# Out stages of an attention and MLP kernel: score tiles in 16 bursts of three and two in place of 18 of two, two and three

## The chip, the cores and the metric

The kernel runs on one core of a Trainium2 chip. The metric is the device time of one execution in microseconds (us); a time given for a kernel is the median of its runs. TensorE does the matmuls, ScalarE (ACT) the activations, VectorE (DVE) elementwise work, GpSimd (POOL) mainly issues loads, and the queue of SyncE (SP) issues transposes and stores. Each engine takes its instructions in program order and waits for others by semaphores. Matmul results land in PSUM, which has eight banks.

## What is computed

Sigmoid attention over 8 batches and 12 heads (448 rows, head size 64), and behind it a two-layer MLP with a SiLU over the 3584 rows of width 768:

```python
scores = scale * np.matmul(q, k.transpose(0, 1, 3, 2)) - np.log(S)
attn = 1.0 / (1.0 + np.exp(-scores))
attn_out = np.matmul(attn, v)
x = attn_out.transpose(0, 2, 1, 3).reshape(B * S, H * D)
h = x @ w_in                                # 768 -> 2048
g = h * (1.0 / (1.0 + np.exp(-h)))
return g @ w_out                            # 2048 -> 768
```

## The kernel before

Four heads of one batch make a group, so there are 24 groups (`g`), three to a batch. A group has seven score tiles (`NCH`), and a tile is one row block of 64 rows of k for four heads: `scores(g, ch)` (L218) issues four 64x64 matmuls of 448 columns, one on each quadrant of the array, into a pair of PSUM banks `psc`, and one sigmoid of ScalarE (L232) takes the pair out to `attnT` in SBUF. Two heads share a bank on its two partition halves. The sigmoids of a group's seven tiles are then multiplied with its values: `values(g)` (L240) issues 28 matmuls of the same small kind into a pair of banks `pav`, and VectorE takes the pair out with two `tensor_scalar_mul` (L267), one for each bank. These are called the two scales below.

The program goes: the first 24 tiles with transposes and values; the first MLP layer of batches 0 and 1 with tiles 24 to 41 in it; then for m = 0, 1, 2 an out stage and an h stage; and a last out stage without scores. An out stage `sets(m)` multiplies the hidden rows of batches 2m and 2m+1 with `w_out`. Each set is seven products of eight dense 128x128 matmuls of 384 columns (L504), by a Strassen-like scheme with sums `S` and evictions on VectorE (L512 to L539). There are three sets in stages 0 and 2 and four in stage 1 (and in the last). In between these dense matmuls the out stage computes all 42 score tiles and five of the six values products for the next two batches. The sixth values product (of the group that ends with the stage's last tile) stands at the beginning of the h stage, `h_pair`, which multiplies the new rows with `w_in`.

The order of TensorE's work in an out stage is fixed when the program is built. `burst(n, size)` (L738) issues `size` score tiles in a row and behind them, if a group is complete and waiting, its values. A group is put on `waiting` after the burst that holds its seventh tile, so its values come with the next burst. Then comes a number of dense matmuls taken from the stream `sets(m)`. The planner keeps a running sum `left` in ns: each burst adds its share of the stage's planned time and takes off its own cost (200 for a burst, `SWITCH`, 200 for each tile, 1330 for values), and the rest is filled with dense matmuls at 163 each, at least one:

```python
left += total * size / (2 * NT_B) - SWITCH - TILE * size - VALUES * burst(n, size)
count = max(1, round(left / DENSE))
```

With sizes 2, 2, 3 in turn (L773), seven tiles take three bursts; every complete group ends with a burst of three, and the values go along with the next burst of two. After each burst and again in the middle of its dense matmuls `rows_if_any` (L589) may issue one further step of side work: a VectorE copy and a transpose on SP's queue for the k or q of a later group, or a sum over x.

PSUM in these stages (`banks_for_attention(3)`, L766) is three double pairs, taken in turn, and two single banks for the dense products (`po`). Score tiles and the values' `pav` both take the next double pair (`two_banks`, L96). `reuse_waits="tile"` in `new_pool` makes the first write to a pair wait for the readers of the tile that had it before.

Of the kernel before, what the change touches and what calls it, by code (L numbers as in the profile page):

```python
# [17 lines left out]
def kernel(  # L18
# [18 lines left out]
    NQ = NPAIR // 2  # L37
    NT_B = NQ * NCH
# [25 lines left out]
    def banks_for_attention(doubles):  # L64
        psum.close()
        banks.clear()
        bufs_of.update(double=doubles, single=NBANK - 2 * doubles)
        for name, bufs in bufs_of.items():
            taken[name] = 0
            new_pool(name, bufs)  # L70
# [7 lines left out]
    def banks_for_h():  # L78
        doubles = [[2 * i, 2 * i + 1] for i in longest_idle("double")]
        ring[:] = sum(doubles[:-2], [])  # L80
        ring.extend(2 * bufs_of["double"] + i for i in longest_idle("single"))
        ring.extend(sum(doubles[-2:], []))
        psum.close()
        banks.clear()
        new_pool("any", 1)
        for i in range(NBANK):
            banks[i] = banks["any"].tile([P, 512], F32, tag=f"any{i}", name=f"any{i}")
# [130 lines left out]
    def scores(g, ch):  # L218
        attnT[g, ch] = p12.tile([P, 2, S], F16, tag="attnT", name="attnT")
        psc = two_banks("psc")  # L220
        for half in range(2):
            own = slice(half * HP, (half + 1) * HP)
            for j in range(2):
                rows = slice(j * D, (j + 1) * D)
                nc.tensor.matmul(  # L225
                    psc[own, j, :S],
                    qkT["k", g][rows, ch, own],
                    qkT["q", g][rows, :, own],
                    start=True,
                    stop=True,  # L230
                )
        nc.scalar.activation(attnT[g, ch], psc[:, :, :S], AF.Sigmoid, bias=bias_s, scale=QKSCALE)  # L232
# [7 lines left out]
    def values(g, end=NCH):  # L240
        b, iq = divmod(g, NQ)
        if b not in xT:
            assert b < 2 or b - 2 in h_done
            xT[b] = p2.tile([P, NPAIR, S], F16, tag="xT", name="xT")
        pav, done_rounds = part_of.pop(g, None) or (None, 0)
        if pav is None and bufs_of["double"] > 2 and "any" not in banks:
            both = two_banks("pav")
            pav = [both[:, half] for half in range(2)]
        elif pav is None:
            pav = [one_bank("pav") for _ in range(2)]  # L250
        for ch in range(done_rounds, end):
            at = attnT.pop((g, ch))
            for half in range(2):
                own = slice(half * HP, (half + 1) * HP)
                for j in range(2):
                    nc.tensor.matmul(  # L256
                        pav[half][j * D : (j + 1) * D, :S],
                        flat["v", g][own, j, ch, :],
                        at[own, j, :],
                        start=(ch == 0),  # L260
                        stop=(ch == NCH - 1),
                    )
        if end < NCH:
            part_of[g] = pav, end
            return
        for half in range(2):
            nc.vector.tensor_scalar_mul(xT[b][:, half * NQ + iq, :], pav[half][:, :S], SX)  # L267
        if iq == NQ - 1:
            ready.add(b)
# [75 lines left out]
    def x_sums(m, lo, hi):  # L345
        if lo == 0:
            for i in (1, 2, 4):
                tx[m, i] = room_x()
        of = slice(lo, hi)
        x0, x1 = ([xT[2 * m + j][:, c * NQ : (c + 1) * NQ] for c in range(2)] for j in range(2))  # L350
        for o, x, y in (
            (tx[m, 1], x1[0], x0[0]),
            (tx[m, 2], x1[1], tx[m, 1]),
            (x1[0], x1[1], x1[0]),
            (tx[m, 4], x0[1], tx[m, 2]),
        ):
            nc.vector.tensor_sub(o[:, of], x[:, of], y[:, of])
            yield
# [211 lines left out]
    def sets(m):  # L570
        for g in range(0, NCH - 1, 2):
            step = out_set(
                block(m, g), row_blocks(m, g), block(m, g + 1), row_blocks(m, g + 1)
            )
            for i, ns in enumerate(step):
                if m == 0 and g == 0 and i in (10, 14):
                    next(sums)
                if m == 0 and g == 0 and i in (20, 28, 36, 44):
                    next(in_sums)
                yield ns  # L580
        if m % 2 == 1:
            g = NCH - 1
            yield from out_set(
                kept, row_blocks(m - 1, g), block(m, g), row_blocks(m, g), m == B // 2 - 1
            )
# [3 lines left out]
    def rows_if_any(before, copy):  # L589
        if sums_of_x and next(sums_of_x[0], "end") == "end":  # L590
            sums_of_x.pop()
        if later and later[0][0] < before:
            g, name = later.pop(0)
            dma_transpose(g, name, copy)
            if name == "q":
                behind_rows(g, before)
# [48 lines left out]
    def after_values(g):  # L645
        if g == 0:
            load("v", 3)
            load_w_in(2)
            load_w_in(3)
        elif g == 1:  # L650
            load("v", 4)
            load_w_out(0, 0)
            load_w_out(0, 1)
        elif g == 2:
            load("v", 5)
            load_w_out(1, 0)
            load_w_out(1, 1)
            load("kq", 6)
            load("kq", 7)
        elif g + 3 < NQB:  # L660
            load("v", g + 3)
        if g >= 2 * NQ and g % (2 * NQ) == 2 * NQ - 2:
            sums_of_x.append(x_sums(g // (2 * NQ), 0, NQ - 1))

    def values_if_any():
        if waiting:
            g = waiting.pop(0)
            values(g)
            after_values(g)
            return True  # L670
        return False
# [66 lines left out]
    def burst(n, size=2):  # L738

        new = units[n : n + size]  # L740
        for u in new:
            scores(*u)
        with_values = values_if_any()
        for g, ch in new:
            if ch == NCH - 1:
                waiting.append(g)
                if 9 <= g + 3 < NQB:
                    later.extend(((g + 3, "k"), (g + 3, "q")))
        return with_values
# [3 lines left out]
    for n in range(NT_B + 3, 2 * NT_B, 2):  # L753
        burst(n)
        if n in (26, 30):
            transposes(5, "k" if n == 26 else "q")
        stretch(stream, 1600)
# [6 lines left out]
    SWITCH, TILE, VALUES, DENSE = 200, 200, 1330, 163  # L764
    for m in range(B // 2 - 1):
        banks_for_attention(3)  # L766
        nc.scalar.activation(warm, bias_s, AF.Sigmoid)
        stream = sets(m)
        for _ in range(FIRST_DENSE):
            next(stream)  # L770

        dense = (3 + m % 2) * 7 * NHC - FIRST_DENSE - ENDING
        sizes = [2, 2, 3]  # L773
        costs = sum(SWITCH + TILE * size for size in sizes) * 2 * NQ + VALUES * (2 * NQ - 1)
        total = dense * DENSE + costs
        own = 2 * NQ * (m + 2)
        left, n = 0.0, 2 * NT_B * (m + 1)
        for size in sizes * (2 * NQ):
            left += total * size / (2 * NT_B) - SWITCH - TILE * size - VALUES * burst(n, size)
            n += size  # L780
            rows_if_any(own, nc.vector.tensor_copy)
            count = max(1, round(left / DENSE))
            left -= count * DENSE
            half = count // 2
            for i in range(count):
                next(stream)
                if i == half:
                    rows_if_any(own, nc.vector.tensor_copy)
        assert not sums_of_x
        nc.scalar.activation(warm, bias_s, AF.Silu)  # L790
        for _ in stream:
            pass
        (g,) = waiting
        waiting.clear()
        banks_for_h()
        values(g, NCH - 1)

        def last_values():
            values(g)
            after_values(g)  # L800
            for _ in x_sums(m + 1, NQ - 1, NQ):
                pass
            nc.gpsimd.tensor_copy(gate, tx[m + 1, 4][:1, NQ - 1, :1])

        for i, _ in enumerate(h_pair(m + 1, last_values)):
            if i % 8 == 7:
                rows_if_any(NQB, nc.gpsimd.tensor_copy)
# [33 lines left out]
```

## Time and profile before

| | us |
|---|---|
| median of 3 runs | 369.92 (369.61 to 370.37) |
| the profiled execution | 369.69 |
| its span, first to last instruction | 367.7 |
| out stage 0 (m = 0), to the first matmul of the h stage | 48.4, from 75.57 |
| out stage 1 (m = 1) | 57.1, from 156.27 |
| out stage 2 (m = 2) | 48.5, from 245.61 |
| last out stage, without scores | 41.1, from 326.6 |

In the profile a line of the timeline has start and duration in us, the engine, the line of the kernel, the operation, what it writes and reads, its size, and how many such instructions in a row were merged; in brackets is the idle time ahead of it and what ended that. A matmul's record is longer than the distance to the next one's start (dense ones last 0.33 us in the records and follow each other after 0.163), so how long a stretch takes is read from starts. The costliest groups of the three out stages in the table of groups are the sigmoids (168 of 1009 ns, over the whole kernel), the dense products `po` and the score matmuls `psc`; the scales are 48 instructions of 620 ns over the whole kernel, of which each of the three out stages has ten.

### The profile page before, as it was taken

How to read it: one execution, taken by the hardware profiler on the slowest of the kernel's cores; microseconds unless marked ns; L12 is line 12 of the kernel's file. 1: busy time of each engine (PE TensorE's matmuls, PEld its weight loads, DVE VectorE, ACT ScalarE, POOL GpSimd, SP SyncE). 2: the span in 40 equal slices, each digit the busy share in tenths (PEclk: the TensorE clock that was granted, in tenths of full speed). 3: DMA queues.
4: the chain of work that ended last, by engine and by line, in shares of the span. 5: the costliest groups of instructions: out<-in, count | busy, mean ns of one | idle time of the engine just before them, and what ended most of it. 6: DMA issues, size and time to landing. Idle time of an engine off the chain costs nothing. (4 is left out here: it accounts for less than half of the span.)

```text
span 367.7 us, 7596 instructions
## 1 busy us (share of the span) xinstructions
PE 359.5 (98%) x3009; PEld 183.2 (50%) x3009; DVE 251.9 (68%) x458; ACT 249.9 (68%) x339; POOL 77.8 (21%) x116
## 2 busy tenths in 40 slices
PE   7999999999999999999999999999999999999995
PEld 2554445545544555544444545554455545555553
DVE  2565569867657587867665758795756667797763
ACT  5998885479998755687777846679998856640000
POOL 8566521040060172000051047000100000000000
PEclk9999999999999999999999999999999999999999
DMA  8999999989969499007589369912863020003333
GB/s 142 200 202 202 204 204 203 187 116 141 164 100 227 110 128 180 2 0 166 92 165 206 61 128 144 128 15 51 153 111 86 21 69 0 3 0 86 87 86 86
DMA packets 65698, 42.78 MB, mean 116 GB/s; under 512 B 36096, under 2 KB 62208, under 8 KB 65664
## 3 DMA queue, kind: packets, MB, share of 16 engines
q0 software_dynamic: 27072, 22.58, 42.3%
q1 hardware_dynamic: 38240, 19.44, 26.8%
q8 instruction: 23, 0.38, 0.4%
q10 hardware_dynamic: 352, 0.30, 0.2%
q14 instruction: 11, 0.09, 0.1%
HBM read 45.61 MB, written 11.01 MB: 154 GB/s over the span
## 5 line engine op out<-in xcount | busy, mean ns | idle before, releaser
L232 ACT ACTIVATE attnT<-psc,bias_s 128x896 f16<-128x896 f32 x168 | 158.1, 1009 | 21.9 <-PE psc L225 21.6
L504 PEld LDWEIGHTS <-S 128*128 128x128 f16 x448 | 41.3, 98 | 36.5 <-issue 8.1
L225 PE MATMUL psc<-qT,kT 64*64 64x448 f16 x672 | 51.1, 362 | 1.5 <-ACT qT L186 0.6
L267 DVE TENSOR_SCALAR xT<-pav 128x448 f16<-128x448 f32 x48 | 27.7, 620 | 33.2 <-PE pav L256 33.2
L124 POOL DMA_DIRECT2D vf<-in_v_dram x24 | 17.2, 717 | 135.0 <-PE pav L256 120.9
L504 PEld LDWEIGHTS <-gTr 128*128 128x128 f16 x336 | 31.3, 98 | 26.6 <-issue 7.7
L504 PE MATMUL po<-T,S 128*128 128x384 f16 x224 | 42.0, 327 | 0.2 <-DVE S L515 0.2
L504 PE MATMUL po<-w_out_sb,gTr 128*128 128x384 f16 x224 | 41.6, 327 | 0.0
L378 PEld LDWEIGHTS <-w_in_sb 128*128 128x128 f16 x288 | 27.7, 98 | 26.9 <-issue 1.7
L504 PE MATMUL po<-w_out_sb,S 128*128 128x384 f16 x224 | 40.8, 326 | 0.0
L256 PE MATMUL pav<-attnT,vf 64*64 64x448 f16 x672 | 38.9, 350 | 0.5 <-DVE gTr L303 0.4
L288 PE MATMUL ph<-xT,w_in_sb 128*128 128x448 f16 x192 | 38.7, 353 | 0.1
L378 PE MATMUL pa<-xT,w_in_sb 128*128 128x448 f16 x144 | 33.2, 353 | 0.0
L225 PEld LDWEIGHTS <-kT 64*64 64x64 f16 x672 | 17.8, 104 | 28.8 <-issue 22.3
L378 PEld LDWEIGHTS <-SI 128*128 128x128 f16 x216 | 21.1, 98 | 20.0 <-issue 0.5
L256 PEld LDWEIGHTS <-vf 64*64 64x64 f16 x672 | 21.0, 106 | 14.0 <-issue 4.7
L288 PEld LDWEIGHTS <-w_in_sb 128*128 128x128 f16 x192 | 17.8, 98 | 19.1 <-issue 3.7
L394 ACT ACTIVATE part<-pa 128x448 f32<-128x448 f32 x24 | 13.1, 544 | 19.9 <-PE pa L378 19.0
L504 PE MATMUL po<-T,gTr 128*128 128x384 f16 x112 | 22.1, 327 | 0.0
L372 ACT ACTIVATE gTr<-pc 128x448 f16<-128x448 f32 x24 | 13.1, 544 | 12.9 <-DVE pc L388 12.5
L388 DVE TENSOR_TENSOR part<-pb,part 128x448 f32<-128x448 f32 x24 | 14.9, 621 | 8.3 <-ACT part L394 5.0
L186 ACT ACTIVATE m<-po 128x384 f32<-128x384 f32 x1 | 0.5, 491 | 27.7 <-PE po L504 27.7
(75 smaller groups left out, 467.7 us busy)
## 6 DMA issues: line engine op xcount, KB each, us to landing
out_dram<-osb SPq DMA_DIRECT2D x54, 192.0 KB, 3.0
vf<-in_v_dram POOLq DMA_DIRECT2D x24, 224.0 KB, 7.0
kf<-in_k_dram POOLq DMA_DIRECT2D x23, 224.0 KB, 7.7
qf<-in_q_dram POOLq DMA_DIRECT2D x23, 224.0 KB, 7.9
w_in_sb<-in_moe_w_in_dram POOLq DMA_DIRECT2D x16, 192.0 KB, 8.2
w_out_sb<-in_moe_w_out_dram POOLq DMA_DIRECT2D x4, 768.0 KB, 14.9
kT<-kr SPq DMA_TRANSPOSE x18, 4.1
qT<-qr SPq DMA_TRANSPOSE x18, 4.8
```

The source lines that it names most:

```text
L124: nc.gpsimd.dma_start(flat[name, g][:, :, c0:c1].rearrange("p i c d -> p i (c d)"), rows_in(name, g)[:, :, c0 * D : c1 * D],)
L186: nc.scalar.activation(o, i, AF.Copy)
L225: nc.tensor.matmul(psc[own, j, :S], qkT["k", g][rows, ch, own], qkT["q", g][rows, :, own], start=True, stop=True,)
L232: nc.scalar.activation(attnT[g, ch], psc[:, :, :S], AF.Sigmoid, bias=bias_s, scale=QKSCALE)
L256: nc.tensor.matmul(pav[half][j * D : (j + 1) * D, :S], flat["v", g][own, j, ch, :], at[own, j, :], start=(ch == 0), stop=(ch == NCH - 1),)
L267: nc.vector.tensor_scalar_mul(xT[b][:, half * NQ + iq, :], pav[half][:, :S], SX)
L288: nc.tensor.matmul(ph[:, :S], w_in_sb[:, cc, fc * P : (fc + 1) * P], xT[b][:, cc, :], start=(at == 0), stop=(at == NCC - 1),)
L372: nc.scalar.activation(gTr[:, r * NG + i, col + c * S : col + (c + 1) * S], h, AF.Silu, bias=0.0, scale=ISX)
L378: nc.tensor.matmul(to, w[:, n, i * P : (i + 1) * P], x[:, n], start=(start and n == 0), skip_group_check=not start, stop=(n == NQ - 1),)
L388: nc.vector.tensor_add(o, po, x)
L394: nc.scalar.activation(got[i, 1], bank[i, "a"], AF.Copy)
L504: nc.tensor.matmul(po[:, :NO2], a[:, fc, :], w[:, fc, :], start=(fc == 0), stop=(fc == NHC - 1))
```

## The change

The sizes of the bursts in an out stage are written out for the whole stage: ten bursts of three and six of two, 16 in all, across the limits of the groups. The complete groups' last tiles lie in bursts 3, 5, 8, 11, 13 and 16; the values go along with bursts 4, 6, 9, 12 and 14, which are bursts of two, and each of these five is followed by a burst of three. An assertion in `burst` says that values go along with two tiles alone. The planner's costs count 16 bursts in place of 18; its constants and its rule are the same, and so are all matmuls, activations and copies in number.

```diff
@@ burst
         with_values = values_if_any()
+        assert not with_values or size == 2
@@ out stage
         dense = (3 + m % 2) * 7 * NHC - FIRST_DENSE - ENDING
-        sizes = [2, 2, 3]
-        costs = sum(SWITCH + TILE * size for size in sizes) * 2 * NQ + VALUES * (2 * NQ - 1)
+        sizes = [3, 3, 3, 2, 3, 2, 3, 3, 2, 3, 3, 2, 3, 2, 3, 2]
+        assert sum(sizes) == 2 * NT_B
+        costs = sum(SWITCH + TILE * size for size in sizes) + VALUES * (2 * NQ - 1)
         total = dense * DENSE + costs
         own = 2 * NQ * (m + 2)
         left, n = 0.0, 2 * NT_B * (m + 1)
-        for size in sizes * (2 * NQ):
+        for size in sizes:
```

## The prediction

> **What bounds the kernel now.** I read the page first, for the share of each engine, then the windows over the three stages that the change touches, then the timeline of TensorE inside such a stage, and then the timeline of all engines around one values product.
>
> ```profile
> PE 359.5 (98%) x3009; PEld 183.2 (50%) x3009; DVE 251.9 (68%) x458; ACT 249.9 (68%) x339; POOL 77.8 (21%) x116
> ...
> 75.57:123.98 48.41, 48.41 (x501) 24.53 (x499) 33.21 (x61) 43.21 (x47) 11.41 (x17) 1.00 0.89 146
> 156.27:213.32 57.05, 56.90 (x558) 28.20 (x556) 38.32 (x70) 43.93 (x49) 8.41 (x12) 1.00 0.61 114
> 245.61:294.14 48.53, 48.53 (x502) 24.47 (x500) 32.07 (x58) 43.87 (x49) 2.15 (x3) 1.00 0.42 80
> ```
>
> TensorE is busy all through, at a granted clock of 1.00 in these stages, and the chain of waits that ended last is TensorE work almost alone. The three windows are the out stages: length first, then the busy time of TensorE, weight load, VectorE, ScalarE and GpSimd, the granted clock, and the DMA. A busy TensorE hides short waits, because a matmul record here is longer than its pitch, so starts have to be compared. Whatever TensorE loses or gains in these windows goes into the end time one for one.
>
> The price of a burst comes from two undisturbed ones of the second out stage:
>
> ```profile
> 156.27 2.44 PE L504 MATMUL po<-w_out_sb,gTr 128*128 128x384 f16 x14
> 158.64 0.57 PE L225 MATMUL psc<-qT,kT 64*64 64x448 f16 x8
> 159.15 0.50 PE L504 MATMUL po<-w_out_sb,gTr 128*128 128x384 f16 x2
> ...
> 162.82 0.98 PE L504 MATMUL po<-T,gTr 128*128 128x384 f16 x5
> 163.72 0.76 PE L225 MATMUL psc<-qT,kT 64*64 64x448 f16 x12
> 164.42 0.66 PE L504 MATMUL po<-T,gTr 128*128 128x384 f16 x3
> ```
>
> Eight score matmuls are two tiles, twelve are three. A dense matmul follows the last after 0.163 us (2.44 less one record of 0.33, over 13). So the two-tile burst costs 159.15 - 156.27 - 14 x 0.163 = 0.60, and the three-tile burst 164.42 - 162.82 - 5 x 0.163 = 0.79. That gives 0.19 for a tile and 0.22 for the burst itself. Of the burst, 0.09 lies ahead of its first matmul, and from there to the next dense matmul it is 0.51 (two tiles) or 0.70 (three).
>
> The stretch around a values product in the third out stage:
>
> ```profile
> 262.44 0.57 PE L225 MATMUL psc<-qT,kT 64*64 64x448 f16 x8
> ...
> 262.84 1.49 PE L256 MATMUL pav<-attnT,vf 64*64 64x448 f16 x28
> 262.93 1.91 ACT L232 ACTIVATE attnT<-psc,bias_s 128x896 f16<-128x896 f32 x2 [0.39 <-PE psc L225]
> ...
> 264.27 0.34 PE L504 MATMUL po<-w_out_sb,gTr 128*128 128x384 f16 x1
> 264.39 1.16 DVE L267 TENSOR_SCALAR xT<-pav 128x448 f16<-128x448 f32 x2 [1.04 <-PE pav L256]
> ...
> 264.53 0.74 PE L225 MATMUL psc<-qT,kT 64*64 64x448 f16 x8
> ...
> 265.21 0.66 PE L504 MATMUL po<-w_out_sb,gTr 128*128 128x384 f16 x3
> ...
> 267.11 2.81 ACT L232 ACTIVATE attnT<-psc,bias_s 128x896 f16<-128x896 f32 x3 [0.17 <-PE psc L225]
> ```
>
> After the values there is one dense matmul and at once the next burst. Its body is 265.21 - 264.53 = 0.68 and not 0.51: the second tile waits 0.17 until ScalarE has emptied its banks (262.93 + 1.91 = 264.84). VectorE's two scales empty the values' banks from 264.39 to 265.55. Those banks are next wanted by the first tile of the three-tile burst, at 266.61, a whole 1.06 us later. That distance is what the change takes away.
>
> **The change part by part.** *Fewer bursts.* 18 become 16 in each of three stages, with the same 42 tiles, values and dense matmuls: 6 x 0.22 = -1.32 us.
>
> *Old waits that go.* The two-tile bursts after values in the first and third out stage have bodies of 0.61, 0.67, 0.67, 0.68, 0.67 and 0.61, 0.68, 0.67, 0.68, 0.68 by their starts (0.51 undisturbed): 0.75 + 0.77. Three three-tile bursts there are above 0.70 by 0.10, 0.16 and 0.05. In all 1.83 us; the second out stage has none. They all disappear, or are contained in the new wait below: -1.83.
>
> *The new wait.* Three double banks A, B, C go round in turn. Before, a group of seven tiles took 2 + values, 2, 3, which is eight banks, so the values' pair was followed by two other pairs before it came up again. Now every burst with or without values takes exactly A, B, C: scores in A and B, values in C, and the burst right behind it, three tiles, takes C for its third tile. In the changed program's order the first matmul of that third tile holds a wait on VectorE's second scale, behind all five values of each stage. Reckon from the dense matmul behind the values (264.27 above). The next burst begins at +0.26, its third tile would begin at +0.26 + 2 x 0.19 = +0.64. The scales begin at +0.12, take 1.16, and the word of VectorE reaches TensorE some 0.06 later (estimate: from the end of ScalarE's 264.84 to the weight load that waited for it, 264.89, 0.05; and 0.07 in the second stage between a VectorE sum's end and the product that waited for it). So the third tile begins at +1.34: a wait of 0.70. How many dense matmuls follow a burst is fixed at build time by the planner's running sum `left`, which charges 1330 ns for the values: still a single one behind each of the five in the first and third out stage: 10 x 0.70 = 7.0. The second has three dense matmuls there four times, and four once. Its rows put the burst at +0.59 (from 177.94 to 178.53) and +0.76 (from 169.11 to 169.87), so the third tile is due at +0.97 and +1.14 and waits 0.37 and 0.20: 4 x 0.37 + 0.20 = 1.68. Added: +8.68. TensorE takes its work in order, so the dense matmuls behind the tile are all late with it; the product evictions and S sums of VectorE behind the scales are no later relative to them.
>
> This rests on VectorE being free when the values end. In the rows of before it had idled 0.7 to 2.4 us ahead of nearly all scales. In the new order the VectorE work ahead of each pair is at most an eviction, an S sum and a copy for a transpose (0.56 + 0.68 + 0.61 = 1.85), whose product ended at least before the burst that carries the values, 0.40 + 1.42 = 1.8 us. I take no delay, and keep up to 0.61 (one more piece) at a few of the fifteen for the upper end.
>
> The Trainium skill speaks against this edit: Perfetto Trace Analysis, Optimizing Tensor Performance (Matmuls), has independent matmul groups rotate through different PSUM banks, so that one is evacuated under the next one's matmuls. Here the rotation continues but falls in step with the bursts. The trace agrees as to the old order (the 1.06 us above); the page prices nothing, so by it only the sign follows.
>
> *ScalarE in rows of three.* The first eviction starts 0.49 after a burst's first matmul (262.44 to 262.93) and three take 2.81, with 0.06 for the word to TensorE; so the third pair is free at +3.36. With 13 dense matmuls the next burst starts at 0.70 + 13 x 0.163 + 0.09 = +2.91 and wants it at +3.29: 0.07 late once per such stage, and 0.04 late once ahead of values. With 14 there is no wait, and behind a stalled burst there is slack. +0.22 over the first and third stage; the bounds are 0 and 0.24 for each of some four bursts with 12 or 13 dense matmuls, 2 us in all. In the second stage there are 17 or 18 and none waits.
>
> *The moved calls.* The 36 places per stage at which copies for transposes and sums of x are issued become 32, all still ahead of their need: a group's k and q copies follow its predecessor's last tile by no more than a burst, with some 10 us before the scores that read them, and the transposes land in 4 to 5 us. SP's and POOL's queues get the same issues in the same order: 0, covered by those 10 us; if the cover were gone, one landing (4.8) would be exposed.
>
> Sum: -1.32 - 1.83 + 8.68 + 0.22 = **+5.75 us**. The profiled execution took 369.69 (span 367.7 and 2.0 around it), which gives 375.4; the median of the runs is 0.23 above it, so I say **375.6 us**.
>
> **The rivals.** *The faster side: the third tile is let in after the first scale.* A tile's first matmul writes the first bank of the pair, the second scale only reads the other. If the wait really ended there, at +0.12 + 0.62 + 0.06 = +0.80, it would cost 0.16 ten times and nothing in the second stage: -1.32 - 1.83 + 1.6 + 0.22 = -1.3, 368.6 us. It decides as soon as the fifteen waits total under 2.9 us instead of 8.7. For it: the halves lie in different banks. Against it: the wait in the built order is on the second scale. 5%.
>
> *The loss is half given back.* TensorE's pauses let VectorE and ScalarE catch up, and waits inside dense stretches (0.15 on an S sum in the second stage) vanish, or the third tile's weights and queue start sooner. With 0.50 instead of 0.70: 2 to 3 us less, 373. Against it: dense stretches show hardly any wait to be given back. 10%.
>
> *VectorE comes late to the scales.* One piece of 0.61 at each of five values: +3.1, 378.7 us; at all fifteen 384.8. For it: VectorE is busy two thirds of these stages (33.21 of 48.41 us in the first) and the copies stand close. Against it: the idle time ahead of the scales. 10%.
>
> *A burst removed saves nothing*, because the 0.22 is from two rows and may belong to the tiles: 376.9, inside the range; 5%.
>
> **How the numbers follow.** The forecast itself, 374 to 377.5, has 67%. What is left, 3%, is that losses and gains cancel. The range takes in the half loss and the VectorE case at five values: 372.5 to 379. A difference of 0.2% (0.74 us) is about what a measurement of this kernel tells from none: faster by more 5%, within it 3%, slower 92%.
>
> **What would show it.** In the timeline after, each burst behind values has twelve score matmuls over some 1.4 us to the next dense matmul in the first and third out stage, and 0.9 to 1.1 in the second, with VectorE's scale named as the releaser of the third tile; the three windows grow by about 2.3, 1.2 and 2.2 us; all other three-tile bursts have bodies near 0.70. I am wrong if these bodies are near 0.7 to 0.8, or if the windows grow elsewhere, in the dense products or between the stages.

## The result and the profile after

The changed kernel takes 375.51 us (median of 4 runs, 375.05 to 375.68), the kernel before 370.02 in the same comparison: a ratio of 1.0147 (95% interval 1.0135 to 1.0159), 5.49 us slower. The forecast was 375.6.

The windows of the three out stages in the profile after, with the same columns as before:

```profile
76.00:126.77 50.77, 49.04 (x501) 24.21 (x500) 33.28 (x61) 43.00 (x47) 11.15 (x17) 1.00 0.82 139
159.06:216.96 57.90, 57.23 (x558) 28.52 (x556) 38.45 (x70) 43.71 (x49) 8.04 (x12) 1.00 0.64 112
249.24:300.01 50.77, 49.10 (x502) 24.29 (x500) 32.06 (x58) 43.71 (x49) 2.14 (x3) 1.00 0.41 76
```

Against 48.41, 57.05 and 48.53 they are longer by 2.36, 0.85 and 2.24 us, 5.45 together; the forecast had 2.3, 1.2 and 2.2. The span grew by 5.9 (373.6 against 367.7): the remaining 0.43 is there before the first out stage, which begins at 76.00 and not 75.57. It arises in the first 7 us, in code that did not change (the first score matmul starts at 7.03 and not 6.60); in the profiles of all versions here, which do not differ up to that stage, its start lies between 75.17 and 76.19.

The timeline of all engines around one values product and the burst behind it in the third out stage, from the profile after:

```profile
275.21 0.57 PE L225 MATMUL psc<-qT,kT 64*64 64x448 f16 x8
...
275.61 1.49 PE L256 MATMUL pav<-attnT,vf 64*64 64x448 f16 x28
275.70 1.91 ACT L232 ACTIVATE attnT<-psc,bias_s 128x896 f16<-128x896 f32 x2 [0.27 <-PE psc L225]
...
277.04 0.34 PE L504 MATMUL po<-w_out_sb,S 128*128 128x384 f16 x1
277.16 1.16 DVE L267 TENSOR_SCALAR xT<-pav 128x448 f16<-128x448 f32 x2 [1.29 <-PE pav L256]
...
277.30 0.74 PE L225 MATMUL psc<-qT,kT 64*64 64x448 f16 x8
...
278.37 0.38 PE L225 MATMUL psc<-qT,kT 64*64 64x448 f16 x4 [0.32 <-DVE xT L267]
278.68 1.90 PEld L504 LDWEIGHTS <-S 128*128 128x128 f16 x13 [0.20 <-issue]
278.68 2.29 PE L504 MATMUL po<-w_out_sb,S 128*128 128x384 f16 x13
```

The burst begins at 277.30. Its third tile starts at 278.37, 1.33 us behind the dense matmul of 277.04, and the bracket names VectorE's scale, which ends at 277.16 + 1.16 = 278.32. The bracket gives only 0.32 us of idle time, because the records of the two tiles ahead (277.30 + 0.74) cover the beginning of the wait; by starts the third tile is 1.07 into the burst, where 0.40 is usual. The burst's body is 278.68 - 277.30 = 1.38. The list of waits of TensorE shows the same thing by its brackets:

```profile
PE psc L225 <- DVE xT L267: 4.1, 14, 0.4
```

Before, that pair was not in the list at all. Fourteen of the fifteen bursts behind values are in it; the fifteenth, with four dense matmuls ahead, has a wait so short that the records hide it.

### The profile page after: what moved, and what is told of

Read it like the earlier page. It is cut to its first block, busy times and chain, and to the rows that moved or that the text cites. A ratio compares the mean times of both kernels' runs of the same rounds, so it can differ in the third digit from the quotient of the medians.

```text
span 373.6 us, 7600 instructions
## 1 busy us (share of the span) xinstructions
PE 361.5 (97%) x3009; PEld 183.4 (49%) x3009; DVE 252.1 (67%) x458; ACT 249.5 (67%) x339; POOL 77.5 (21%) x116
## 4 chain that ended last, share of the span: by engine, by line
PE 83%; DMA 6%; DVE 5%; issue 2%; ACT 1%; POOL 0%; SPq 0%; DVEq 0%; ACTq 0%
PE po L504 33%; PE psc L225 8%; PE pa L378 7%; PE pd L378 7%; PE pc L378 7%; PE pav L256 7%; PE ph L288 6%; DMA w_out_sb<-in_moe_w_out_dram 5%; PE pb L378 4%; DVE xT L267 3%; PE pw L183 2%; DMA out_dram<-osb 1%; DVE kT L203 1%; ACT attnT L232 1%; DVE qT L203 0%
## 5 line engine op out<-in xcount | busy, mean ns | idle before, releaser
L225 PE MATMUL psc<-qT,kT 64*64 64x448 f16 x672 | 52.4, 363 | 5.5 <-DVE xT L267 4.1
L124 POOL DMA_DIRECT2D kf<-in_k_dram x25 | 18.1, 725 | 4.8 <-DMA vf<-in_v_dram 2.1
```

The source lines that it names most:

```text
L124: nc.gpsimd.dma_start(flat[name, g][:, :, c0:c1].rearrange("p i c d -> p i (c d)"), rows_in(name, g)[:, :, c0 * D : c1 * D],)
L225: nc.tensor.matmul(psc[own, j, :S], qkT["k", g][rows, ch, own], qkT["q", g][rows, :, own], start=True, stop=True,)
```

## The experiments

The forecast's theory is that the new order makes the third tile behind values wait for the pair of banks that VectorE is just emptying, since three pairs of banks are all that there is. Each expectation says anew what its own theories A and B are. The runs of each version are compared with runs of the kernel before on the same chip; its median was 369.96 to 370.17 in these.

### Dense matmuls moved behind the values

```diff
-            left += total * size / (2 * NT_B) - SWITCH - TILE * size - VALUES * burst(n, size)
+            with_values = burst(n, size)
+            left += total * size / (2 * NT_B) - SWITCH - TILE * size - VALUES * with_values
...
-            count = max(1, round(left / DENSE))
+            count = max(5 + m % 2 if with_values else 1, round(left / DENSE))
```

> The changed kernel with at least five dense matmuls behind each values product in out stages 0 and 2 and six in out stage 1, in place of one, and three or four; the bursts are the same, and the dense matmuls come out of the gaps behind. Theory A (the three pairs of banks turn round too slowly in rows of three, wherever the dense matmuls stand): the waits on VectorE's scale vanish, and in stages 0 and 2 waits on ScalarE's sigmoids of 0.7 to 0.9 us take their place where 8 or 9 dense matmuls follow a burst of three (3.4 us a stage, against 3.6), so these stages stay at 50.4 to 50.8 us; stage 1 has the room and falls by 1.6 to 56.3. In all 373.4 us. Theory B (it is only the place of the dense matmuls: moved behind the values, they cover the scales at no cost): 366.8 us.

Measured: 372.42 us (ratio 1.0065, 1.0050 to 1.0080). The windows, and two places of TensorE's timeline in the third stage:

```profile
76.19:126.26 50.07, 48.12 (x501) 24.03 (x500) 33.11 (x61) 42.42 (x47) 11.25 (x17) 1.00 0.85 141
158.55:214.79 56.24, 56.24 (x557) 28.61 (x556) 38.37 (x70) 43.67 (x49) 8.07 (x12) 1.00 0.65 116
247.08:297.09 50.01, 48.12 (x502) 24.10 (x500) 31.88 (x58) 43.13 (x49) 2.14 (x3) 1.00 0.45 77
```

```profile
263.67 0.57 PE L225 MATMUL psc<-qT,kT 64*64 64x448 f16 x8
264.67 1.52 PE L256 MATMUL pav<-attnT,vf 64*64 64x448 f16 x28 [0.42 <-ACT attnT L232]
...
269.16 0.71 PE L225 MATMUL psc<-qT,kT 64*64 64x448 f16 x8
270.38 0.38 PE L225 MATMUL psc<-qT,kT 64*64 64x448 f16 x4 [0.51 <-ACT attnT L232]
```

The waits on the scale are gone, and waits on ScalarE stand in their place: the values begin 1.00 us after their burst's start where 0.40 is usual, and a third tile comes at 1.22. Over a stage the new waits come to 2.8 us, where theory A had 3.4. Stages 0 and 2 gain only 0.70 and 0.76 us (theory A had 0 to 0.4, and 373.4 us in all); stage 1, which has four sets' dense matmuls to spread, gains 1.66 and has no wait between bursts left. Theory B's 366.8 us is out.

### Short scales, in both orders

The two scales of batches 2 to 7 are cut to 64 columns, in the changed kernel and in the one before; so part of the attention's result is left out:

```diff
+            if b >= 2:
+                nc.gpsimd.memset(xT[b], 0.0)
...
+            n = S if b < 2 else 64
-            nc.vector.tensor_scalar_mul(xT[b][:, half * NQ + iq, :], pav[half][:, :S], SX)
+            nc.vector.tensor_scalar_mul(xT[b][:, half * NQ + iq, :n], pav[half][:, :n], SX)
```

> The changed kernel, in which the two scales of batches 2 to 7 take 64 of the 448 columns out of PSUM (the rest of the rows is zeros, written by GpSimd), so that part of the attention's result is left out. Theory A (the loss is the wait for the scales): the wait of the third tile goes, 7.0 and 1.7 us, and the second tile's wait on ScalarE, as in the kernel before, shows again, 10 x 0.17: 368.5 us. Theory B (the loss is from three tiles in a row for ScalarE, or from VectorE's queue in general): 373 us or more.

> The kernel before with the same short scales (64 of 448 columns for batches 2 to 7, the rest zeros, so part of the attention's result is left out). Theory A: nothing waits for the scales in the order 2 with values, 2, 3, so the time stays within 0.5 us of the kernel before, 369.5 to 370.2 us. Theory B (VectorE's load as such costs TensorE time): 368.5 us or less.

Measured: 371.97 and 371.14 us. Both totals miss both theories, since the added zeros did harm of their own in stage 0. The windows of stages 1 and 2, free of it, for the changed order and then for the order before:

```profile
159.39:215.64 56.25, 56.25 (x557) 28.55 (x556) 34.63 (x70) 43.67 (x49) 10.65 (x14) 1.00 0.67 116
247.93:296.05 48.12, 48.12 (x501) 24.02 (x500) 28.22 (x58) 43.67 (x49) 4.79 (x5) 1.00 0.45 80
```

```profile
157.66:214.38 56.72, 56.72 (x557) 28.29 (x555) 34.57 (x70) 43.89 (x49) 10.65 (x14) 1.00 0.62 115
246.67:295.16 48.49, 48.49 (x501) 24.49 (x499) 28.08 (x58) 43.83 (x49) 4.79 (x5) 1.00 0.42 80
```

With short scales the changed order's stages fall from 57.90 and 50.77 to 56.25 and 48.12, by 1.65 and 2.65; theory A had 1.68 and, with the second tile's 0.17 coming back five times, 7.0/2 - 0.85 = 2.65. The order before moves by 0.33 and 0.04 (57.05 and 48.53 to 56.72 and 48.49), although VectorE has the same 4 us less to do; the 0.33 is a wait on an S sum inside a dense stretch that has gone (0.15 of it shows as idle time before), and no burst became shorter. So in these stages the loss is in the wait for the scales and not in VectorE's load or the rows of three; without that wait the 16 bursts are the faster order, by 0.47 and 0.37 us. In stage 1 no wait between bursts is left in either order. In stage 2 both still have waits on ScalarE behind values, of 0.10 to 0.17 us.

What spoilt stage 0 is GpSimd's fill, which stood behind its load issues and came late. From the timeline of the changed order with short scales:

```profile
110.45 2.40 POOL L246 MEMSET xT<- 128x2688 f16 x1
...
112.89 0.35 DVE L270 TENSOR_SCALAR xT<-pav 128x64 f16<-128x64 f32 x2 [3.50 <-POOL xT L246]
113.30 0.38 PE L225 MATMUL psc<-qT,kT 64*64 64x448 f16 x4 [1.85 <-DVE xT L270]
```

### 18 bursts with a burst of three behind the values

```diff
-        sizes = [3, 3, 3, 2, 3, 2, 3, 3, 2, 3, 3, 2, 3, 2, 3, 2]
+        sizes = [2, 3, 2] * (2 * NQ)
```

> 18 bursts as before, but in the order 2, 3, 2, so that a burst of three follows each values product directly. Theory A (the loss is from three tiles right behind the values, not from the number of bursts): the 18 bursts cost what they did, the old waits of 1.8 us go, and the new one of 0.70 shows ten times and 0.2 to 0.4 five times: 376.7 us. Theory B (the loss is from bursts of three following each other, or from the groups' limits lying inside the bursts): within 0.5 us of the kernel before, 370 us.

Measured: 376.42 us (1.0173, 1.0156 to 1.0190), 0.3 under theory A. Two lines of TensorE's timeline in the third stage:

```profile
261.40 0.68 PE L225 MATMUL psc<-qT,kT 64*64 64x448 f16 x8
262.46 0.38 PE L225 MATMUL psc<-qT,kT 64*64 64x448 f16 x4 [0.38 <-DVE xT L267]
```

The number of bursts is that of the kernel before, and the groups end at the end of a burst as they do there; only the places of a two and a three are exchanged, and the third tile again starts 1.06 into its burst. The order alone makes the loss; the two bursts less are not its cause.

### That order with dense matmuls behind the values, alone and with 16 bursts in stage 1

```diff
-        sizes = [3, 3, 3, 2, 3, 2, 3, 3, 2, 3, 3, 2, 3, 2, 3, 2]
+        sizes = [2, 3, 2] * (2 * NQ)
...
-            count = max(1, round(left / DENSE))
+            count = max(5 + m % 2 if with_values else 1, round(left / DENSE))
```

In the second of the two runs the sizes of stage 1 are those of the changed kernel.

> The order 2 with values, 3, 2 in 18 bursts, with at least five dense matmuls behind the values in out stages 0 and 2 and six in stage 1. By the turnaround of the pairs (2.78 us from a burst with values to a following burst of three, 2.27 from three to two, 2.06 from two to two with values: 7.11 for seven tiles, against 7.16 of TensorE's own work) no wait over 0.05 us is left in any out stage. Theory A: the old waits of 1.8 us are gone and ten of 0.05 come in: 368.7 us. Theory B (each shortening of one gap brings a wait elsewhere, as ScalarE has no room): 370 us or more.

> As the run before in out stages 0 and 2, and in stage 1 the changed kernel's 16 bursts with at least six dense matmuls behind the values. Theory A: stage 1 has room for both (3.6 us between bursts of three, where 2.98 are needed) and saves two bursts of 0.22: 0.4 us less than that run, 368.2 us. Theory B (a burst less saves nothing, as the 0.22 belongs to the tiles): the same as that run.

Measured: 371.39 us (1.0036, 1.0023 to 1.0048) and 370.50 (1.0012, 1.0003 to 1.0021). The first is 2.7 us over theory A's 368.7, on theory B's side, and the second, with the same stages 0 and 2, 2.3 us over its 368.2. The third stage of the first shows why:

```profile
262.95 0.57 PE L225 MATMUL psc<-qT,kT 64*64 64x448 f16 x8
263.73 1.52 PE L256 MATMUL pav<-attnT,vf 64*64 64x448 f16 x28 [0.21 <-ACT attnT L232]
```

The values start 0.78 into the burst, 0.38 late, four times a stage. I had reckoned each pair of bursts by itself, as if ScalarE began every burst fresh. With 9 dense matmuls on both sides of the two-tile burst it does not: the last sigmoid of the group, which the values read, stands in its queue behind the three of the burst before. So in this order the time that five dense matmuls give to the scales is taken from ScalarE later. The second run's 0.9 us less than the first is mainly stage 1 (56.97 to 56.24 us, 0.73); of that 0.24 is less waiting inside the dense stretches, and the rest, 0.49, goes with the two bursts less. Theory A had 0.4, B none.

### One scale in place of two

```diff
-            pav = [both[:, half] for half in range(2)]
+            pav = [both[:, half] for half in range(2)] + [both]
...
-        for half in range(2):
-            nc.vector.tensor_scalar_mul(xT[b][:, half * NQ + iq, :], pav[half][:, :S], SX)
+        if len(pav) == 3:
+            to = xT[b].rearrange("p (h q) s -> p h q s", h=2)[:, :, iq]
+            nc.vector.tensor_scalar_mul(to, pav[2][:, :, :S], SX)
...
```

> The changed kernel with the two scales of a values product in the out stages as one VectorE instruction of 128x896. Theory A (each of the fifteen waits ends with the scales): 1.16 us for the two becomes some 1.08 (0.15 fixed and 0.467 for 448 elements, from a mean of 620 ns and a distance of 0.54 between the two starts), 15 x 0.08 = 1.2 us less than the changed kernel, 374.3 us. Theory B (the wait ends with the first scale or with something else): the time is the same, or more by the longer single instruction, 375.5 us or above.

Measured: 374.80 us (1.0129, 1.0114 to 1.0145), 0.7 less than the changed kernel, where theory A had 1.2. The single instruction, from the answer for the tile `pav`:

```profile
L268 DVE TENSOR_SCALAR xT<-pav x15: 1091/1092/1093, 89.5 to 290.8; 128x896 f16<-128x896 f32 x15
```

1.092 in place of 1.16 is 0.07 us, and each of the three stages is 0.32 to 0.33 shorter, 0.065 for each of its five waits, about 1.0 in all (theory A had put the instruction at 1.08, and 0.08 for each wait): the wait ends with the end of the scales, to the size. A wait on the first half alone would have become longer by this edit.

> The run with 2, 3, 2 in out stages 0 and 2, 16 bursts in stage 1 and dense matmuls behind the values, and with one scale in place of two. Theory A: the waits on the scales of up to 0.05 us in ten bursts go, 0 to 0.5 us less than without it, 367.9 us. Theory B: no difference, 368.2 us.

This is the same edit in the second run of the test above. Measured: 370.31 us against 370.50, with ranges that overlap (369.81 to 370.88, 369.78 to 370.86): no difference to be told. In its third stage the bursts of three behind values shorten from 0.72 or 0.73 to 0.69, and the next values wait on ScalarE that much longer (they begin 0.81 into their burst in place of 0.78 or 0.79). Where the waits are on ScalarE, a shorter scale is worth nothing.

### Gaps by hand, and the best of both

```diff
+        mixed = [3, 3, 3, 2, 3, 2, 3, 3, 2, 3, 3, 2, 3, 2, 3, 2]
+        sizes = mixed if m % 2 else [2, 2, 3] * (2 * NQ)
+        by_hand = [] if m % 2 else [7, 10, 14, 2, 9, 14, 3, 9, 14, 3, 9, 14, 2, 9, 14, 3, 9, 1]
...
+            count = max(6 if with_values else 1, round(left / DENSE))
+            if by_hand:
+                count = by_hand.pop(0)
```

The second run has the 16 sizes in all stages, with gaps 13, 13, 14, 5, 13, 5, 13, 13, 3, 11, 13, 3, 11, 6, 9, 1 in stages 0 and 2; the third has no gaps by hand, the planner's own for stages 0 and 2. Stage 1 is in all three that of the run with 2, 3, 2 and 16 bursts.

> Out stages 0 and 2 with the 18 bursts of the kernel before, their gaps written out by hand: 1 dense matmul behind the last burst in place of 14 (8 more and the next values' first six tiles follow there anyway), and the 13 go to the gaps that had waits, 2 or 3 behind values and 9 between two and three tiles. Stage 1 as in the run with 2, 3, 2 and 16 bursts. Theory A (a gap is worth something only between two bursts that share the banks; the ones behind the last burst are idle room): all waits of 0.85 and 0.98 us go, stages 0 and 2 fall to 47.5, stage 1 stays at 56.2; 367.3 us. Theory B (ScalarE has no room, and waits come back elsewhere): stages 0 and 2 at 48.4 or above, 369.2 us or more.

> The changed kernel's 16 bursts in all three stages, with the gaps of stages 0 and 2 by hand: again 1 behind the last burst, 3 to 6 behind values, 9 to 14 elsewhere, and at least six behind values in stage 1. Theory A (16 bursts are not slow in themselves, but they leave little room: 2.98 us between two bursts of three, 2.78 from values to three): waits of 0.4 us twice and some of 0.05 are left, 1.0 in all, against 3.6; stages 0 and 2 at 48.2, 368.6 us. Theory B (rows of three over the groups' limits lose time whatever the gaps): stages 0 and 2 at 50 or above, 372 us as with five behind the values.

> Out stages 0 and 2 as in the kernel before, stage 1 with the changed kernel's 16 bursts and at least six dense matmuls behind values. Theory A (two bursts less are worth 0.44 us where nothing waits, and 0.3 us of waits on S sums go): 0.8 us less than before, 369.2 us. Theory B (nothing is saved by fewer bursts): 370.0 us.

Measured: 369.49 us (0.9984, 0.9975 to 0.9993), 370.11 (0.9996, 0.9988 to 1.0005) and 369.11 (0.9972, 0.9961 to 0.9983), where theory A had 367.3, 368.6 and 369.2. In the first every wait between bursts is gone, and stages 0 and 2 still take 48.63. The wait has moved to the stage's end:

```profile
289.33 1.64 PE L504 MATMUL po<-w_out_sb,S 128*128 128x384 f16 x9
...
291.98 1.33 PE L256 MATMUL pav<-attnT,vf 64*64 64x448 f16 x24 [1.02 <-ACT attnT L232]
```

The dense matmuls behind the last burst were not idle room: the next values' first matmul starts just behind the end of the stage's last sigmoid (at 291.93), although the tile that it reads was ready long before; which of its dependencies holds it is not shown. The second run has the same wait, of 0.74 us. Still, it shows that 16 bursts in all stages need not cost 5.5 us: with gaps set to fit, its stages 0 and 2 take 48.90 and 48.88 us in place of 50.77 each, and what they still lose against the kernel before (0.84 together) stage 1 makes up (56.25 against 57.05). The third, with 16 bursts in stage 1 alone, where there is room, is as expected, and faster than both kernels. Its stage 1 against the 57.05 of before:

```profile
156.78:213.02 56.24, 56.24 (x557) 28.59 (x555) 38.37 (x70) 43.71 (x49) 8.07 (x12) 1.00 0.68 116
```

The last run goes back to 18 bursts in stages 0 and 2 and gaps by hand, and keeps six dense matmuls behind the last burst; against the first of the three:

```diff
-        by_hand = [] if m % 2 else [7, 10, 14, 2, 9, 14, 3, 9, 14, 3, 9, 14, 2, 9, 14, 3, 9, 1]
+        by_hand = [] if m % 2 else [6, 10, 14, 2, 9, 14, 2, 9, 14, 2, 9, 14, 2, 9, 14, 2, 8, 6]
```

> As the run with gaps by hand and 18 bursts, but with 6 dense matmuls behind the last burst in place of 1 (with the 8 that follow, 2.3 us), because in that run the next values' first matmul waited 1.02 us for the stage's last sigmoid. Theory A (three pairs and ScalarE leave room for all but some 0.7 us of waits, wherever the dense matmuls stand: 0.15 in the last burst of three, 0.3 to 0.4 at the end, 0.1 to 0.2 in the first): stages 0 and 2 at 48.1, 0.4 less than in the kernel before, stage 1 at 56.2, 368.4 us. Theory B (the planner's gaps are as good as any): stages 0 and 2 at 48.4 to 48.6, 369.1 us.

Measured: 368.45 us (0.9954, 0.9941 to 0.9968), as theory A had it (368.4), and the fastest version here, 1.7 us under the kernel before and 7.1 under the changed one. Its windows:

```profile
75.96:123.94 47.98, 47.79 (x502) 24.21 (x500) 32.90 (x61) 42.90 (x47) 11.95 (x18) 1.00 0.95 148
156.22:212.46 56.24, 56.24 (x557) 28.58 (x555) 38.37 (x70) 43.72 (x49) 8.04 (x12) 1.00 0.66 116
244.76:292.83 48.07, 47.88 (x502) 24.17 (x500) 31.92 (x58) 43.62 (x49) 2.15 (x3) 1.00 0.46 81
```

## Why the prediction was right

The forecast said 5.75 us, and 5.49 was measured; its terms can be read one by one in the profile after. That 375.51 lies within 0.1 us of the forecast 375.6 is in part luck: the change is 0.26 smaller, and the kernel before was 0.10 slower in this comparison than the median from which the forecast was made.

- *The new wait*, +8.68: the ten bursts behind values in stages 0 and 2 have bodies of 1.38 where 0.70 is undisturbed, 6.8 against 7.0; the five in stage 1 have 1.05, 1.06, 1.05, 0.89 and 1.06, that is 1.6 against 1.68. In all 8.4. That it is the scales is shown by the bracket, by the short scales (1.65 and 2.65 us gone from stages 1 and 2, and from the order before only the 0.33 of a wait inside a dense stretch) and by the single scale (0.065 a wait).
- *The switches*, -1.32: in stage 1 with short scales, where neither order has a wait between bursts and the waits inside the dense stretches are alike, two bursts less are worth 0.47 us; 0.44 was forecast. In stage 2 the difference of 0.37 still holds waits of both orders (about 1.2 and 1.1 us by starts); without them it is some 0.45. The rival by which they save nothing is out.
- *The old waits*, -1.83: the two-tile bursts that had them no longer exist. The second tile behind values still comes up to 0.16 late, inside the new wait, as forecast.
- *ScalarE in rows of three*, +0.22: overstated. Bursts of three with 13 dense matmuls ahead have bodies of 0.69 to 0.70, and what is left is some 0.06 at the fourth values of stages 0 and 2.
- *Not in the sum*: waits inside the dense stretches, by starts that are over 0.163 apart. They went from 0.15, 0.54 and 0.15 to 0.34, 0.23 and 0.34 us. That stage 1 grew by 0.85 and not 1.24 is 0.31 of this. It is the rival of the half loss, at a small part of its size, and in the total it is nearly undone by what the other two stages gained in waits of this kind (0.19 each): luck, as the sum had neither.

A stage then closes: for stage 0, -0.44 - 0.85 + 3.4 + 0.06 + 0.19 = +2.36, as measured. The faster rival, a wait for the first scale alone, is out by the body of 1.38 (it had 0.86) and by the run with one scale. VectorE did not come late: each pair of scales began 0.12 behind the first dense matmul, as before.

What the forecast did not say is how far the wait can be bought off inside stages 0 and 2. Moving dense matmuls behind the values alone turned it into waits on ScalarE; with all gaps set by hand, 1.9 us of the 2.2 to 2.4 that each of these stages had lost came back. My expected totals were 1.5 to 2.7 us too low for the three runs with 2, 3, 2 and moved dense matmuls, where I had reckoned bursts two at a time, and for the first two with gaps by hand, where I had taken the stage's end for free.

## What to carry to other kernels

When work is regrouped into larger bursts, count how many buffers each burst takes against the ring it draws from: when the counts fall in step, a slow reader's buffer comes up in the very next burst. A saved switch of 0.22 us is worth having only where the gaps are longer than the turnaround of the buffers: here the 16 bursts with six dense matmuls behind values were right in stage 1 (56.24 against 57.05 us), and in stages 0 and 2 no version of them with the whole result beat the kernel before. A gap that a planner leaves may be holding back a queue, not idling; here moving it showed that.

## What the runs showed of the hardware

In the changed order with short scales TensorE began no matmul in stage 0 between about 111.1 and 113.30. The windows around that place, in which the column ahead of the last two is the granted clock:

```profile
110.50:113.60 3.10, 1.25 (x17) 0.45 (x13) 0.35 (x2) 2.42 (x3) 3.00 (x3) 1.00 1.10 235
113.60:115.00 1.40, 1.40 (x12) 0.83 (x9) 0.53 (x2) 1.01 (x1) 0.00 (x0) 0.85 1.24 217
115.00:116.90 1.90, 1.90 (x7) 0.68 (x5) 0.77 (x3) 0.00 (x0) 0.00 (x0) 0.50 1.26 203
```

About 1.3 us after the pause the granted clock fell to 0.50, which it kept from 114.6 to 118.0, and dense matmuls followed each other at 0.32 us in place of 0.163. Stage 0 took 51.44 us and stage 2 with the same order 48.12; of these 3.3 us the pause itself is 2.0 (the third tile 2.53 into its burst, 0.49 in the same burst of stage 2), and the other 1.3 are put down to the slow clock behind it. The Trainium skill (TensorE: Matmul & The Clock Gate, Part 1) names an idle window of about 3.4 us ahead of the half clock; here a pause of 2.2 us was followed by it. The pauses of 0.7 us in the changed kernel left the clock at 1.00 in all three windows. So did the pause for the same fill in the order before with short scales, where no matmul began between 110.66 and 112.37. How long a pause has to be for the clock to fall, and whether its place in time matters, these runs do not show.
